# Planning the lists with loads in issue order and eight in flight, and giving twelve subtractions of the weight split to GpSimd

## The chip, the cores and the metric

The kernel runs on one NeuronCore of a Trainium2 chip. Its engines are TensorE (PE, with its weight loads as PEld), VectorE (DVE), ScalarE (ACT), GpSimd (POOL) and SyncE (SP), each with its own in-order list of instructions; they wait for each other through semaphores. SP issues most DMAs, POOL the loads of the attention's values. The metric is the device time of one execution in microseconds (us); the median of several runs is compared.

## What is computed

Attention in chunks, then two MLPs, all in float32:

```
chunk, left, right = 32, 16, 8          # q, k, v: 4 x 8 heads x 768 x 64; 8 memory rows
for each chunk c:
    k_full = [mem_k, k[c - left : c + chunk + right]];  v_full likewise
    a = softmax(q_c @ k_full.T / 8);    out_c = a @ v_full
x = out as 3072 x 512
g = s * relu(x @ w_in)**2 + b           # w_in 512 x 2048
x = g @ w_out                           # w_out 2048 x 512
y = (silu(x @ w_gate) * (x @ w_val)) @ w_out2   # 512 x 1536, 512 x 1536, 1536 x 512
```

## The kernel before, in words

**Tiles.** The 3072 tokens are eight tiles of 384 (t = 0 to 7), each made by three attention groups of 128 queries (g = 0 to 23). The first MLP's hidden width is cut into 16 slots (m). A slot is 128 columns of w_in and the 128 rows of w_out that belong to them, 1 MB in two DMAs (`load_slot`, lines 264 and 269), issued by SP.

**Exact products.** A float32 product is made of three fast ones: each operand is split into a high part and a rest (hi, lo), and `product` (lines 701 to 703) adds hi*hi, hi*lo and lo*hi. Splitting a slot (`split`, line 976) takes a chain of six: absolute value (`t_first`, ACT at line 985 or DVE at 987), bound (DVE, 991), shift (DVE, 995), sign (DVE, 1000), rest (DVE, 1007), the rounded copy hi (ACT or DVE, line 253 or 255), and the subtraction lo (`lo`, DVE, line 1049). All work on 128 x 1024 elements.

**The work by name.** The string START (line 30) orders PE's first work, one letter a piece: Q and K turn queries and keys of the first six groups, S makes scores, A turns probabilities (tile psA), V multiplies by values (psV), X turns the normalised result "on" (psO) into xhi and xlo, U is one slot's first product (hp) and D its second (acc). Each U or D is 12 matmuls of 384 columns. The pairs (t, m) of U and D go by SEGMENTS: m 0 to 3 of t = 0, then m 0 to 7 of t = 1, then the rest. So the fifth U, called U4 below, is the first of t = 1, and needs X3, X4 and X5, its groups' results.

**The planner.** The kernel writes its own schedule: `Plan.run` (line 116) plays the tasks against each other with the costs written beside them, and the order of starts in that play becomes the order of each engine's instructions. The chip then keeps that order and waits where a semaphore says so. Three tables feed it: START; LOADS (line 44), which chains the issues of the loads (BK and BQ keys and queries of the first groups, W slots, K6_n pieces of keys and queries for group 6); and MOVED (line 48), names of tasks that go to the second of their two engines (`either`, line 946: m_first is the absolute value, h_first hi, and so on).

A load is two tasks (`transfer`, line 953): the issue on SP and a transfer of so many kilobytes at a rate. The planner allows two such transfers in flight and starts the most urgent ready one first:

```
issue = issues[name] = plan.add(SP, 0.45 * n, emit, deps, [*get, "fly"], take=take)
return plan.add(MOVE, kilobytes / rate, None, [issue], put=["fly"], lag=1.8, give=give)
```

The values of a group are 8 to 10 DMAs issued by POOL (`load_values`, line 511; planned by `load_v`, line 958). Three buffers hold them in the first six groups: v0 for groups 0 and 3, v1 for 1 and 4, a lent slot "values" for 2 and 5. In the program as built, a DMA of SP waits for the one that stands eight places before it in SP's list, and likewise on POOL.

Of the kernel before, what the change touches and what calls it, by code (L numbers as in the profile page):

```python
# [29 lines left out]
START = (  # L30
    "K0 Q0 S0 Q1 A0 S1 S2 K1 V0 A1 S3 X0 V1 A2 X1 V2 A3 S4 X2 V3 U A4 S5 X3 U V4 A5 D X4 U D V5 "
    "U X5 D U D "
)
# [10 lines left out]
LOADS = (  # L44
    "BK0 C BM BK1 BQ01 BQ00 K6_0 BQ11 BQ10 W1 W0 W2 W3 W7 W4 W5 W12 W6 W8 W10 W9 W14 W11 W13 W15 "
)

MOVED = (
# [12 lines left out]
)  # L61


PAGE, FETCH = 256, ((45.0, 8.3), (110.0, 4.0), (1e9, 2.5))


class Plan:
# [32 lines left out]
    def after(d, t):  # L100

        return d.lag + (0.0 if d.engine == t.engine else 0.25)

    def end(self, t, now):

        left, rest = t.words, t.length
        while left:
            n = min(left, PAGE - self.word % PAGE)
            now, rest, left = now + rest * n / left, rest - rest * n / left, left - n
            self.word += n  # L110
            if self.word % PAGE == 0:
                now = max(now, self.next)
                self.next = now + (next(us for at, us in FETCH if now < at) if self.word > PAGE else 4.0)
        return now

    def run(self):
# [9 lines left out]
        heapq.heapify(events)  # L126
        ready = {t.engine: [] for t in self.tasks}
        free = dict.fromkeys(ready, True)
        started = []
        self.word, self.page, self.next = 0, 0.0, 0.0  # L130
        while events:
# [15 lines left out]
            for engine, waiting in ready.items():  # L147
                for item in sorted(waiting) if free[engine] else ():
                    t = self.tasks[item[1]]
                    if all(self.room[r] >= t.get.count(r) for r in t.get):  # L150
                        for r in t.get:
                            self.room[r] -= 1
                        waiting.remove(item)
                        free[engine] = False
                        t.start = now
                        started.append(t)
                        heapq.heappush(events, (self.end(t, now) if engine == "PE" else now + t.length, 0, t.n))
                        break
# [5 lines left out]
def attention_and_two_mlps(  # L164
# [467 lines left out]
    def stage_probs_copy(engine, g):  # L632
        staged[g]["at"] = at = ap_.tile([P, NC, P], F32, tag="at", name=f"at{g}")
        copy(engine, at, staged[g].pop("a"))
# [26 lines left out]

    def stage_normalise(g, e):
        if e == 0:
            staged[g]["on"] = ap_.tile([P, 4 * 2 * D], F32, tag="on", name=f"on{g}")
# [263 lines left out]
    def second_store(h, s, i):  # L928
# [7 lines left out]
    plan = Plan(  # L936
        dict(w=SLOTS - LENT, wt=SLOTS - 5, fly=2),
        dict(
# [14 lines left out]
    def transfer(deps, emit, n, kilobytes, get=(), take=(), give=(), rate=380.0, name=None):  # L953

        issue = issues[name] = plan.add(SP, 0.45 * n, emit, deps, [*get, "fly"], take=take)
        return plan.add(MOVE, kilobytes / rate, None, [issue], put=["fly"], lag=1.8, give=give)

    def load_v(g):
        first = g < VBUFS(0)
        n = 2 * (len(list(value_pieces(g))) + (first or (g >= EARLY and g % GB < VBUFS(g))))  # L960
        if f"V{g}" in LOADS.split():
# [3 lines left out]
            )  # L965
        else:
            issue = plan.add(
                "POOL", 9.2 if first else 0.65 * n, lambda: load_values(g, nc.gpsimd), [batch_landed["VM"]] if first else [],
                take=[f"vb{g % VBUFS(g)}"],
            )  # L970
            v_ = plan.add(MOVE, 1.8 if first else 2.4, None, [issue], lag=5.0 if first else 2.5)
        for e in range(2 if g >= EARLY and g % GB < VBUFS(g) else 0):
# [3 lines left out]
    def split(landed, raw, key, pool, name, done, put=("w",), sums=False):  # L976
# [176 lines left out]
    def plan_scores(g, t=None):  # L1153
# [34 lines left out]
        return t  # L1188

    def plan_probs(g, early):  # L1190
        ring = f"acc{2 + g % 2}" if early else "a"
# [7 lines left out]
        if g < EARLY:  # L1199
# [3 lines left out]
        at_[g]["at"] = either(  # L1203
            f"a{g}", {ACT: 0.50, DVE: 0.60}, lambda e: stage_probs_copy(e, g), [t], take=["at"],
            give=[ring],
        )

    x_parts = {}
    last_x = [None]

    def plan_values(g, t=None):
        d = at_[g]
        give = ["a"] if t is None else []
        if t is None:
            t = plan.add(
                PE, 1.30 if g < EARLY else 1.00, lambda: stage_values(g), [d["at"], d["v"]], take=["a", "a"],
                give=["at"] + [f"vb{g % VBUFS(g)}"] * (g not in (2, 5)), lag=0.2 if g < EARLY else 0.0,
                words=128,
# [9 lines left out]
        for e in range(2):  # L1228
            t = plan.add(
                DVE, 0.34, lambda e=e: stage_normalise(g, e), [t, d["rc"]], give=[*give, *([f"rc{g % 3}"] if e else [])],  # L1230
                take=["on"] if e == 0 else (),
            )
# [12 lines left out]
    def plan_turn(g):  # L1245
# [3 lines left out]
        if g < EARLY:  # L1249
            turned = plan.add(PE, 0.44, lambda: stage_turn(g), [d["on"]], take=["h"], give=["on"], lag=0.25, words=8)  # L1250
        else:
# [327 lines left out]
```

## Time and profile before

| | |
|---|---|
| median of the runs shown | 1216.6 us (1215.94, 1216.6, 1217.46) |
| the profiled execution | 1218.56 us |
| its span | 1216.8 us |
| PE busy | 1177.5 us, 97% |
| DVE busy | 750.3 us, 62% |
| ACT busy | 508.0 us, 42% |
| POOL busy | 146.5 us, 12% |
| DMA, mean | 144 GB/s |

The busy times are of the profiled execution alone, and its span begins with the first instruction. A row of a timeline gives the start in us from there, the duration, engine, source line, operation, destination and sources, the shape, how many were merged (x), and in brackets the idle time of that engine just before with what ended it. A row's duration can overlap the next one's start a little, as engines overlap the end of one instruction with the beginning of the next; differences of starts are free of this.

### The profile page before, as it was taken

The numbers are of one execution on the slowest core, as the hardware profiler recorded it, in microseconds if no ns is written. First come the engines' busy times: TensorE is split into PE (matmuls) and PEld (weight loads), VectorE is DVE, ScalarE is ACT, GpSimd is POOL, SyncE is SP. The second block draws the span as 40 slices with busy tenths as digits, with TensorE's granted clock in tenths as the row PEclk, the third lists the DMA queues.
The fourth block names the chain that finished last, engine by engine and source line by source line (L and its number), as shares of the span: only waits on it lengthen the run. The fifth ranks groups of instructions, "written<-read, shape, count | busy, mean of one in ns | idle before, by whom it ended". The sixth has DMA issues, their size and how long they took to land.

```text
span 1216.8 us, 23806 instructions
## 1 busy us (share of the span) xinstructions
PE 1177.5 (97%) x9440; PEld 1120.1 (92%) x9440; DVE 750.3 (62%) x1315; ACT 508.0 (42%) x924; POOL 146.5 (12%) x235
## 2 busy tenths in 40 slices
PE   6479999999999999999999999999999999999998
PEld 5379999999999999999999899999999999999997
DVE  6789976555455445444488965569853367743343
ACT  4445553233343433342276545346433234432332
POOL 4750013222222223120000000000000000000000
PEclk8699999999999999999999999999999999999999
DMA  9774235322222222220356265296565386465251
GB/s 296 161 196 135 79 95 105 68 45 65 40 55 66 45 64 48 46 54 2 113 201 231 110 228 216 118 323 251 196 228 216 115 331 248 156 250 207 105 207 52
DMA packets 160987, 175.42 MB, mean 144 GB/s; under 512 B 101276, under 2 KB 130252, under 8 KB 159852
## 3 DMA queue, kind: packets, MB, share of 16 engines
q1 hardware_dynamic: 153580, 162.54, 40.7%
q0 software_dynamic: 7296, 11.37, 4.1%
q8 instruction: 74, 1.21, 0.4%
q14 instruction: 37, 0.30, 0.1%
HBM read 124.85 MB, written 48.76 MB: 143 GB/s over the span
## 4 chain that ended last, share of the span: by engine, by line
PE 85%; SPq 5%; DMA 5%; DVE 4%; issue 1%; ACT 0%; DVEq 0%; ACTq 0%
PE hp L701 7%; PE acc L702 7%; PE acc L701 7%; PE acc L703 6%; PE hp L702 6%; PE hp L703 6%; PE chain_A L702 5%; PE oacc L703 5%; PE oacc L702 5%; PE chain_A L703 5%; PE chain_A L701 5%; PE oacc L701 5%; PE chain_B L701 4%; PE chain_B L703 4%; PE chain_B L702 4%; DMA kin<-in_k_dram 1%
## 5 line engine op out<-in xcount | busy, mean ns | idle before, releaser
L701 PE MATMUL hp<-xhi,w_first 128*128 128x384 f32 x512 | 174.3, 340 | 4.4 <-DVE xhi L255 4.4
L701 PE MATMUL acc<-ghi,w_first 128*128 128x384 f32 x512 | 173.1, 338 | 0.7 <-DVE ghi L754 0.3
L702 PE MATMUL hp<-xlo,w_first 128*128 128x384 f32 x512 | 172.0, 336 | 0.2 <-DVE xlo L696 0.2
L702 PE MATMUL acc<-glo,w_first 128*128 128x384 f32 x512 | 171.6, 335 | 0.6 <-DVE glo L761 0.4
L703 PE MATMUL hp<-xhi,w_first 128*128 128x384 f32 x512 | 171.8, 336 | 0.0
L703 PE MATMUL acc<-ghi,w_first 128*128 128x384 f32 x512 | 171.3, 334 | 0.0
L526 POOL DMA_DIRECT2D v<-in_v_dram x190 | 122.6, 652 | 306.9 <-PE psB L643 286.8
L871 ACT ACTIVATE kept<-chain_A 128x384 f32<-128x384 f32 x144 | 70.8, 492 | 187.4 <-PE chain_A L703 187.0
L702 PE MATMUL chain_A<-ops,hi_up 128*128 128x384 f32 x384 | 130.1, 339 | 0.0
L703 PE MATMUL chain_A<-ops,lo_up 128*128 128x384 f32 x384 | 129.4, 337 | 0.0
L701 PE MATMUL chain_A<-ops,hi_up 128*128 128x384 f32 x384 | 128.4, 334 | 0.9 <-ACT g L884 0.9
L741 DVE SCALAR_TENSOR_TENSOR r<-r,ident 128x384 f32<-128x384 f32 x91 | 55.8, 613 | 110.8 <-ACT r L730 110.2
L703 PE MATMUL oacc<-w_down,glo 128*128 128x512 f32 x288 | 114.6, 398 | 0.4 <-DVE glo L896 0.4
L702 PE MATMUL oacc<-w_down,ghi 128*128 128x512 f32 x288 | 113.9, 396 | 0.0
L730 ACT ACTIVATE r<-hp 128x384 f32<-128x384 f32 x94 | 46.1, 490 | 161.8 <-PE hp L703 156.0
L701 PE MATMUL oacc<-w_down,ghi 128*128 128x512 f32 x288 | 112.2, 390 | 0.2 <-ACT ghi L253 0.2
L701 PEld LDWEIGHTS hp<-xhi,w_first 128*128 128x128 f32 x512 | 96.5, 189 | 6.0 <-ACT t_first L985 4.7
L701 PEld LDWEIGHTS acc<-ghi,w_first 128*128 128x128 f32 x512 | 96.1, 188 | 2.0 <-DVE ghi L754 0.7
L702 PEld LDWEIGHTS acc<-glo,w_first 128*128 128x128 f32 x512 | 96.1, 188 | 1.8 <-DVE glo L761 1.0
L702 PEld LDWEIGHTS hp<-xlo,w_first 128*128 128x128 f32 x512 | 96.7, 189 | 0.7 <-DVE xlo L696 0.7
L876 DVE TENSOR_TENSOR kept<-chain_B,kept 128x384 f32<-128x384 f32 x48 | 26.7, 557 | 114.2 <-PE chain_B L703 114.2
L703 PEld LDWEIGHTS hp<-xhi,w_first 128*128 128x128 f32 x512 | 96.6, 189 | 0.0
(170 smaller groups left out, 2247.7 us busy)
## 6 DMA issues: line engine op xcount, KB each, us to landing
ops<-ops_dram SPq DMA_DIRECT2D x56, 768.0 KB
ops_dram<-ops SPq DMA_DIRECT2D x28, 768.0 KB
sum_dram<-o SPq DMA_DIRECT2D x48, 256.0 KB
v<-in_v_dram POOLq DMA_DIRECT2D x162, 56.0 KB, 3.0
raw_first<-in_moe_w_in_dram SPq DMA_DIRECT2D x16, 512.0 KB
raw_first<-in_moe_w_out_dram SPq DMA_DIRECT2D x16, 512.0 KB
o<-sum_dram SPq DMA_DIRECT2D x8, 1024.0 KB
y_dram<-y SPq DMA_DIRECT2D x32, 192.0 KB
```

What stands on the lines that cost most here:

```text
L526: queue.dma_start(out=tv[p0 + row:p0 + row + rows, c].rearrange("p (j d) -> p j d", d=D), in_=v[b, e:H:2, first:first + rows, :].rearrange ...
L701: nc.tensor.matmul(o, whi, xhi, start=first, stop=False, skip_group_check=onto)
L702: nc.tensor.matmul(o, whi, xlo, start=False, stop=False, skip_group_check=onto)
L703: nc.tensor.matmul(o, wlo, xhi, start=False, stop=last, skip_group_check=onto)
L730: nc.scalar.activation(out=r, in_=hp, func=AF.Relu)
L741: nc.vector.scalar_tensor_tensor(out=r, in0=r, scalar=s_sb, in1=r, op0=ALU.mult, op1=ALU.mult)
L871: nc.scalar.activation(out=t, in_=st2[n]["A"], func=AF.Copy)
L876: nc.vector.tensor_tensor(out=t, in0=st2[n]["B"], in1=kept, op=ALU.add)
```

## The change

- The planner's model: eight lanes for SP's loads instead of two transfers, held until landing; transfers start in the order in which they become ready; slots at 265 instead of 345 KB per us; POOL's values in two halves with lanes of their own; PE's instructions fetched at a cost that depends on the transfers that are waiting.
- START, LOADS and MOVED are written anew; so most orders of the first 150 us move.
- The subtraction lo of a first-MLP slot may go to POOL; MOVED sends twelve of the sixteen there: all but slots 0, 4, 11 and 15.
- In the first six groups, odd groups take their "at" and "on" tiles from buffers that lie idle then, so that two groups have one each; normalising (`stage_normalise`) may go to ACT, which MOVED does for group 0.

```diff
 START = (
-    "K0 Q0 S0 Q1 A0 S1 S2 K1 V0 A1 S3 X0 V1 A2 X1 V2 A3 S4 X2 V3 U A4 S5 X3 U V4 A5 D X4 U D V5 "
-    "U X5 D U D "
+    "Q0 K0 S2 S0 Q1 A0 S1 K1 V0 X0 S3 A1 A2 V1 V2 X1 A3 X2 S4 U S5 A4 U V3 A5 D X3 V4 U X4 V5 D "
+    "X5 U D U D "
 )
 LOADS = (
-    "BK0 C BM BK1 BQ01 BQ00 K6_0 BQ11 BQ10 W1 W0 W2 W3 W7 W4 W5 W12 W6 W8 W10 W9 W14 W11 W13 W15 "
+    "BQ01 BQ00 C BK1 BK0 BM BQ11 W0 K6_0 W2 BQ10 W1 K6_1 W3 K6_2 W4 W11 K6_3 W5 W6 W10 K6_4 W7 "
+    "W8 K6_5 K6_6 K6_7 K6_8 W12 W9 K6_9 K6_10 K6_11 W14 W13 W15 "
 )
 MOVED = (
...
+    "h_second17 h_second4 h_second5 k0_0 k0_2 k0_3 k1_0 k1_3 k2_1 k3_1 k7_0 k8_1 k9_1 l_first1 "
+    "l_first10 l_first12 l_first13 l_first14 l_first2 l_first3 l_first5 l_first6 l_first7 "
...
-PAGE, FETCH = 256, ((45.0, 8.3), (110.0, 4.0), (1e9, 2.5))
+PAGE, FETCH, QUEUED = 256, 3.7, 4.8
...
+    def queued(self, now):
+        rest = max(self.moved - now, 0.0) + sum(self.tasks[n].length for _, n in self.ready.get("MOVE", ()))
+        return min(rest, QUEUED)
...
-                self.next = now + (next(us for at, us in FETCH if now < at) if self.word > PAGE else 4.0)
+                self.next = now + FETCH + self.queued(now)
...
-                for item in sorted(waiting) if free[engine] else ():
+                for item in (list(waiting) if engine == "MOVE" else sorted(waiting)) if free[engine] else ():
...
     def stage_probs_copy(engine, g):
+        if g < EARLY and g % 2:
+            at = ap_.tile([P, H * KC], F32, tag="sc", name=f"at{g}").rearrange("p (c s) -> p c s", c=NC)
...
-    def stage_normalise(g, e):
+    def stage_normalise(g, e, engine="DVE"):
...
+        if engine == "ACT":
+            for j in range(NP):
+                nc.scalar.activation(
+                    out=on[:, (2 * j + e) * D:(2 * j + e + 1) * D], in_=o[:, j], func=AF.Copy, scale=rc[:, j]
+                )
+            return
...
-        dict(w=SLOTS - LENT, wt=SLOTS - 5, fly=2),
+        dict(w=SLOTS - LENT, wt=SLOTS - 5, fly=8, vly=10),
...
-        issue = issues[name] = plan.add(SP, 0.45 * n, emit, deps, [*get, "fly"], take=take)
-        return plan.add(MOVE, kilobytes / rate, None, [issue], put=["fly"], lag=1.8, give=give)
+        lanes = ["fly"] * min(n, 8)
+        issue = issues[name] = plan.add(SP, 0.45 * n, emit, deps, [*get, *lanes], take=take)
+        landed = plan.add(MOVE, kilobytes / rate, None, [issue], lag=1.8, give=give)
+        plan.add("NONE", 0.0, None, [landed], put=lanes)
+        return landed
...
-                "POOL", 9.2 if first else 0.65 * n, lambda: load_values(g, nc.gpsimd), [batch_landed["VM"]] if first else [],
+                "POOL", 0.32 * n, lambda: load_values(g, nc.gpsimd), [batch_landed["VM"]] if first else [], lanes,
...
-        def lo():
+        def lo(engine):
             w = done[key]
-            nc.vector.tensor_tensor(
+            (nc.gpsimd if engine == "POOL" else nc.vector).tensor_tensor(
                 out=w[:, 1], in0=held["f"].bitcast(F32), in1=w[:, 0].bitcast(F32), op=ALU.subtract
             )
...
-        return plan.add(DVE, 1.14, lo, [t], put=put)
+        return either(f"l_{name}", {DVE: 1.14, "POOL": 2.5}, lo, [t], put=put, lag=0.3)
```

What moves is seen best in three lists. The first is POOL's, from the loads for group 2 on. A name's first number is the group or the slot, so `w_first2` is slot 2's split; what follows the underline is a buffer's number. Before:

```order
L526 DMA values_215<-in_v_dram 56x4x64 x4
L526 DMA v0_213<-in_v_dram 56x4x64 x8
L526 DMA v1_431<-in_v_dram 56x4x64 x8
L526 DMA values_215<-in_v_dram 56x4x64 x3
L526 DMA values_215<-in_v_dram 48x4x64
L526 DMA values_215<-in_v_dram 8x4x64
```

With the change:

```order
L538 DMA v0_196<-in_v_dram 56x4x64 x8
L1081 TENSOR_TENSOR w_first1_643<-raw_first1_252,w_first1_643 128x1024
L538 DMA v1_420<-in_v_dram 56x4x64 x8
L538 DMA values_198<-in_v_dram 56x4x64 x3
L538 DMA values_198<-in_v_dram 48x4x64
L538 DMA values_198<-in_v_dram 8x4x64
L538 DMA values_198<-in_v_dram 56x4x64 x3
L538 DMA values_198<-in_v_dram 48x4x64
L538 DMA values_198<-in_v_dram 8x4x64
L1081 TENSOR_TENSOR w_first2_772<-raw_first2_212,w_first2_772 128x1024
L1081 TENSOR_TENSOR w_first3_1005<-raw_first3_394,w_first3_1005 128x1024
```

The subtraction of slot 1 now stands between the loads for groups 3 and 4, and those of slots 2 and 3 behind the ten loads for group 5.

The second is ACT's, around the absolute value of slot 4 and the xhi of group 0 or 1. Before:

```order
L253 ACTIVATE at1_663<-psA1_651 128x512
L985 ACTIVATE t_first4_701<-raw_first4_636 128x1024
L253 ACTIVATE xhi0_712<-psO0_704 128x4x128
L609 ACTIVATE values_215<-values_215 128x512
L985 ACTIVATE t_first5_777<-raw_first5_642 128x1024
L253 ACTIVATE w_first3_803<-raw_first3_352 128x1024
L253 ACTIVATE at2_816<-psA2_787 128x512
```

With the change:

```order
L265 ACTIVATE queries1_153<-psK1_2_555 128x12x56
L689 ACTIVATE on0_634<-psV0_0_592,rc0_456 128x64 x4
L689 ACTIVATE on0_634<-psV0_1_593,rc0_456 128x64 x4
L1017 ACTIVATE t_first4_708<-raw_first4_515 128x1024
L265 ACTIVATE at1_719<-psA1_703 128x512
L265 ACTIVATE at2_722<-psA2_712 128x512
L621 ACTIVATE values_198<-values_198 128x512
L265 ACTIVATE w_first2_772<-raw_first2_212 128x1024
L265 ACTIVATE xhi0_700<-psO1_815 128x4x128
```

Slot 4's absolute value stands behind group 0's normalising now, and slot 5's has left this stretch; it comes five places later, ahead of U0's relu.

The third is SP's, just ahead of slot 4's load. Before, the last nine of its rows there:

```order
L441 DMA kin0_193<-in_mem_k_dram 8x4x32
L432 DMA kin0_193<-in_k_dram 16x4x32
L432 DMA kin0_193<-in_k_dram 8x4x32
L451 DMA kin0_193<-in_k_dram 32x4x32
L455 DMA qt6_194<-in_q_dram 32x4x32
L451 DMA kin0_193<-in_k_dram 32x4x32
L455 DMA qt6_194<-in_q_dram 32x4x32
L264 DMA raw_first4_636<-in_moe_w_in_dram 128x4x256
L269 DMA raw_first4_636<-in_moe_w_out_dram 128x1024
```

With the change:

```order
L281 DMA raw_first3_394<-in_moe_w_out_dram 128x1024
L463 DMA kin0_173<-in_k_dram 32x4x32
L467 DMA qt6_174<-in_q_dram 32x4x32
L463 DMA kin0_173<-in_k_dram 32x4x32
L467 DMA qt6_174<-in_q_dram 32x4x32
L276 DMA raw_first4_515<-in_moe_w_in_dram 128x4x256
L281 DMA raw_first4_515<-in_moe_w_out_dram 128x1024
```

Slot 4 was the sixth slot, with fifteen pieces for group 6 just ahead of it; it is the fifth, with four just ahead. Slot 6 comes later in the list: thirty pieces for groups 6 and 7 follow slot 5 in a row, and then slot 6.

## Rows read from the trace of the kernel before

**Rows 1.** Busy time by stretches, columns as its first line names them.

```profile
core 0: us, PE busy (x) PEld busy (x) DVE busy (x) ACT busy (x) POOL busy (x), PEclk, DMA share, GB/s
0.00:89.00 89.00, 56.09 (x1197) 48.62 (x1197) 66.14 (x121) 40.19 (x95) 54.02 (x89) 0.83 0.84 218
89.00:600.00 511.00, 510.26 (x5035) 501.25 (x5036) 303.23 (x576) 202.59 (x365) 92.51 (x146) 1.00 0.28 66
45.00:53.00 8.00, 0.37 (x2) 0.00 (x0) 5.14 (x10) 2.71 (x4) 4.70 (x8) 0.50 1.00 187
```

**Rows 2.** Timeline of PE: start, us, what it did, idle before and its releaser.

```profile
44.26 1.11 PE L629 MATMUL psA<-ident,turned 128*128 128x128 f32 x4
53.07 1.13 PE L680 MATMUL psO<-ident,on 128*128 128x128 f32 x4 [7.70 <-DVE on L673]
...
72.71 0.63 PE L680 MATMUL psO<-ident,on 128*128 128x128 f32 x4
73.10 0.42 PE L701 MATMUL hp<-xhi,w_first 128*128 128x384 f32 x1
...
75.29 0.33 PE L701 MATMUL acc<-ghi,w_first 128*128 128x384 f32 x1
...
77.46 0.86 PE L643 MATMUL psV<-values,at 64*32 64x64 f32 x64
...
83.75 0.34 PE L703 MATMUL acc<-ghi,w_first 128*128 128x384 f32 x1
88.54 0.41 PE L701 MATMUL hp<-xhi,w_first 128*128 128x384 f32 x1 [4.45 <-DVE xhi L255]
...
92.61 0.34 PE L701 MATMUL acc<-ghi,w_first 128*128 128x384 f32 x1
```

**Rows 3.** Timeline of ACT, the same columns.

```profile
46.15 1.12 ACT L985 ACTIVATE t_first<-raw_first 128x1024 f32<-128x1024 f32 x1 [7.26 <-DMA raw_first<-in_moe_w_out_dram]
...
83.96 1.12 ACT L985 ACTIVATE t_first<-raw_first 128x1024 f32<-128x1024 f32 x1 [8.65 <-DMA raw_first<-in_moe_w_out_dram]
```

**Rows 4.** Timeline of DVE, the same columns.

```profile
47.79 0.69 DVE L696 TENSOR_TENSOR xlo<-psO,xhi 128x512 fp32r<-128x512 f32 x1 [4.73 <-ACT xhi L253]
...
85.11 0.69 DVE L991 TENSOR_SCALAR t_first<-t_first 128x1024 f32<-128x1024 f32 x1 [3.91 <-ACT t_first L985]
...
88.43 0.69 DVE L696 TENSOR_TENSOR xlo<-psO,xhi 128x512 fp32r<-128x512 f32 x1
```

**Rows 5.** Timeline of SyncE's queue (SPq): issues of loads.

```profile
38.58 0.55 SPq L264 DMA_DIRECT2D raw_first<-in_moe_w_in_dram  x1
...
52.36 0.31 SPq L451 DMA_DIRECT2D kin<-in_k_dram  x1
...
63.67 0.42 SPq L451 DMA_DIRECT2D kin<-in_k_dram  x1
...
77.41 0.56 SPq L264 DMA_DIRECT2D raw_first<-in_moe_w_in_dram  x1
```

**Rows 6.** Timeline of POOL.

```profile
1.02 0.29 POOL masks.py:199 TENSOR_SCALAR_AFFINE_SELECT ident<-ident 128x128 f32<-128x128 f32 x1
...
15.23 0.55 POOL L519 DMA_DIRECT2D v<-values  x1 [4.89 <-DMA values<-in_mem_v_dram]
...
52.84 3.48 POOL L526 DMA_DIRECT2D v<-in_v_dram  x5 [0.26 <-issue]
56.51 6.16 POOL L526 DMA_DIRECT2D values<-in_v_dram  x10 [0.19 <-PE psV L643]
```

**Rows 7.** Groups of DVE by line and shape, 0 to 95 us: count | busy us, mean ns.

```profile
L1049 DVE TENSOR_TENSOR w_first<-raw_first,w_first 128x1024 fp32r<-128x1024 f32 x6 | 7.3, 1219 | 0.1
...
L991 DVE TENSOR_SCALAR t_first<-t_first 128x1024 f32<-128x1024 f32 x8 | 5.4, 681 | 3.9 <-ACT t_first L985 3.9
```

**Rows 8.** Line 526, the loads of values on POOL, 0 to 80 us: ns min/median/max.

```profile
L526 POOL DMA_DIRECT2D v<-in_v_dram x52: 531/650/955, 15.8 to 77.5; - x52
...
DMA to landing us min/median/max: 2.1/4.4/8.1
```

More of the change, by code (lines that the diff above doesn't have):

```diff
@@ L126, in run @@
         heapq.heapify(events)
-        ready = {t.engine: [] for t in self.tasks}
+        self.ready = ready = {t.engine: [] for t in self.tasks}
         free = dict.fromkeys(ready, True)
         started = []
-        self.word, self.page, self.next = 0, 0.0, 0.0
+        self.word, self.next, self.moved = 0, 0.0, 0.0
         while events:
@@ L156, in run @@
                         started.append(t)
-                        heapq.heappush(events, (self.end(t, now) if engine == "PE" else now + t.length, 0, t.n))
+                        until = self.end(t, now) if engine == "PE" else now + t.length
+                        if engine == "VMOVE":
+                            until += 0.45 * self.queued(now)
+                        if engine == "MOVE":
+                            self.moved = until
+                        heapq.heappush(events, (until, 0, t.n))
                         break
@@ L632, in stage_probs_copy @@
     def stage_probs_copy(engine, g):
-        staged[g]["at"] = at = ap_.tile([P, NC, P], F32, tag="at", name=f"at{g}")
+        if g < EARLY and g % 2:
+            at = ap_.tile([P, H * KC], F32, tag="sc", name=f"at{g}").rearrange("p (c s) -> p c s", c=NC)
+        else:
+            at = ap_.tile([P, NC, P], F32, tag="at", name=f"at{g}")
+        staged[g]["at"] = at
         copy(engine, at, staged[g].pop("a"))
@@ L966, in load_v @@
         else:
+            lanes = ["vly"] * 5
             issue = plan.add(
-                "POOL", 9.2 if first else 0.65 * n, lambda: load_values(g, nc.gpsimd), [batch_landed["VM"]] if first else [],
+                "POOL", 0.32 * n, lambda: load_values(g, nc.gpsimd), [batch_landed["VM"]] if first else [], lanes,
                 take=[f"vb{g % VBUFS(g)}"],
             )
-            v_ = plan.add(MOVE, 1.8 if first else 2.4, None, [issue], lag=5.0 if first else 2.5)
+            v_ = plan.add("VMOVE", 1.2, None, [issue], put=lanes, lag=2.0)
+            issue = plan.add("POOL", 0.32 * n, None, [issue], lanes)
+            v_ = plan.add("VMOVE", 1.2, None, [issue, v_], put=lanes, lag=2.0)
         for e in range(2 if g >= EARLY and g % GB < VBUFS(g) else 0):
@@ L1188, in plan_scores, with at_ring @@
         return t
+    def at_ring(g):
+        return "own" if g < EARLY and g % 2 else "at"
     def plan_probs(g, early):
@@ L1203, in plan_probs @@
         at_[g]["at"] = either(
-            f"a{g}", {ACT: 0.50, DVE: 0.60}, lambda e: stage_probs_copy(e, g), [t], take=["at"],
+            f"a{g}", {ACT: 0.50, DVE: 0.60}, lambda e: stage_probs_copy(e, g), [t], take=[at_ring(g)],
             give=[ring],
@@ L1209, in attention_and_two_mlps, with on_ring @@
     last_x = [None]
+    def on_ring(g):
+        return "kt" if g < EARLY and g % 2 else "on"
     def plan_values(g, t=None):
@@ L1216, in plan_values @@
                 PE, 1.30 if g < EARLY else 1.00, lambda: stage_values(g), [d["at"], d["v"]], take=["a", "a"],
-                give=["at"] + [f"vb{g % VBUFS(g)}"] * (g not in (2, 5)), lag=0.2 if g < EARLY else 0.0,
+                give=[at_ring(g)] + [f"vb{g % VBUFS(g)}"] * (g not in (2, 5)), lag=0.2 if g < EARLY else 0.0,
                 words=128,
@@ L1228, in plan_values @@
         for e in range(2):
-            t = plan.add(
-                DVE, 0.34, lambda e=e: stage_normalise(g, e), [t, d["rc"]], give=[*give, *([f"rc{g % 3}"] if e else [])],
-                take=["on"] if e == 0 else (),
+            t = either(
+                f"n{g}_{e}", {DVE: 0.34, ACT: 0.80} if g < EARLY else {DVE: 0.34},
+                lambda engine, e=e: stage_normalise(g, e, engine), [t, d["rc"]],
+                give=[*give, *([f"rc{g % 3}"] if e else [])], take=[on_ring(g)] if e == 0 else (),
             )
@@ L1249, in plan_turn @@
         if g < EARLY:
-            turned = plan.add(PE, 0.44, lambda: stage_turn(g), [d["on"]], take=["h"], give=["on"], lag=0.25, words=8)
+            turned = plan.add(PE, 0.44, lambda: stage_turn(g), [d["on"]], take=["h"], give=[on_ring(g)], lag=0.25, words=8)
         else:
@@ L1269, in plan_w1 @@
         if m not in split1:
-            landed = transfer([], lambda: load_w1(m), 2, 1024, ["w", "w"], rate=345.0, name=f"W{m}")
+            landed = transfer([], lambda: load_w1(m), 2, 1024, ["w", "w"], rate=265.0, name=f"W{m}")
             split1[m] = split(landed, raw1, m, lambda: wp, f"first{m}", w1)
```

6 lines of the change are left out of this document (5 added, 1 removed), and 23 rows, old and new, of the table MOVED.

## Prediction

> **What bounds the kernel now.** I read the busy time by stretches first, to see where TensorE (PE) is not full. From 89 us to 600 us it is busy 510.26 of 511 us at full clock; in the first 89 us it is busy only 56.09 [rows 1]. What the change can win or lose lies in those first 89 us: behind them PE works through a fixed list without pause, so each microsecond by which it enters that list earlier comes off the end. The point of entry is U4, the first product of token tile 1, which starts at 88.54 us [rows 2].
>
> Next I read PE's instructions in order of time. Two of its waits are long. From the end of psA at 45.37 it stands until 53.07, 7.70 us, "on" being late on VectorE (DVE); and from 84.09 until 88.54, 4.45 us, xhi being late on DVE [rows 2]. In the first of them the granted clock is 0.50, the 1.2 GHz level, and PE was busy 0.37 of 8 us [rows 1].
>
> Then the same stretches on the engines that PE waits for. ScalarE (ACT) stands idle for 7.26 us before t_first at 46.15 and for 8.65 us before t_first at 83.96, each time for a load of raw_first [rows 3]. These are the absolute values of slots 4 and 6, which stand in ACT's queue before the load has come. Behind the first stands the xhi for which DVE idles 4.73 us; DVE itself idles 3.91 us for the second, with X5's xhi and xlo behind it in its queue [rows 4]. Last, SyncE's queue says why the loads are late: slot 4 is issued at 38.58, behind five other slots and fifteen pieces for group 6, and lands as ACT begins at 46.15; slot 6 is issued at 77.41 and lands by 83.96, 6.55 us later [rows 3, 5]. So PE is held by loads that an in-order queue asks for too soon, not by the load that PE needs next.
>
> **The change, part by part.** The rules of planning cost nothing by themselves: on the chip each load waits for the eighth before it in both programs. What runs differently is the order on each engine, twelve subtractions on GpSimd, four "at" and "on" tiles with buffers of their own, and group 0's normalising on ACT.
>
> *Loads.* Slot 4 is now the fifth slot to be loaded instead of the sixth, with the group 6 pieces between the slots, and its absolute value stands where ACT comes to it after group 0's normalising. I take both ACT stalls as gone: 4.73 + 3.91 = 8.6 us of DVE's idle time, and PE's two waits with them. The second is the closer call. In the change slot 6 is the load behind thirty small pieces, and its absolute value still stands one place ahead of X5's xhi on ACT. If slot 5 lands as late as the second slot of that pair did before (SyncE moves on at 52.36), and the 24 pieces that still wait then follow at the pace of the 23 from there to 63.67, 0.49 us each, slot 6 is issued at 64.2; with 6.55 us it lands at 70.7, and 1.1 + 0.7 + 0.7 us of ACT and DVE (absolute value, xhi at the price of xlo, xlo) put X5's xlo at 73.2 [rows 3 to 5]. That is hidden behind PE's own path (77.9, below) by 4.7 us.
>
> *DVE.* Up to X5's xlo DVE did 121 instructions, 66.14 us, so it idled 22.9 us of the 89 [rows 1, 4]. In the new order there are 112. The difference is four subtractions of slots fewer (4 x 1.22), two passes of the same size fewer (2 x 1.22), two short passes fewer and two rounding copies more, which I price alike (0.68 each; the copy has no row, the short pass is the nearest) [rows 7]; small instructions on both sides about cancel. That is 7.3 us. With 8.6 us of idle time gone X5's xlo would come at 89.1 - 7.3 - 8.6 = 73.2 us, if DVE alone set it.
>
> *GpSimd (POOL).* This is the new wait. POOL issued 56 loads of values between 15.23 and 62.67, at a median of 0.65 us each 36.4 us of work, with 11.0 us of waits for earlier ones to land [rows 6, 8]. Now the subtraction of slot 1 stands between group 3's loads and group 4's, and those of slots 2 and 3 behind the ten loads for group 5. No row shows a subtraction on POOL. Below, it can't be taken to beat DVE's 1.22 us; above, its affine select of 128 columns took 0.29 us [rows 6, 7], eight of those are 2.3 us, and reading two inputs instead of one could double that to 4.6. I take 2.3, the count by the nearest row. The Trainium skill (GPSIMD Engine Reference, Performance versus the Vector engine) has 4497 ns for 2048 columns, so an estimate of 2.25 us by halves; the sum would be the same within 0.1 us a piece.
>
> So slot 1's subtraction (2.3) puts the end of group 5's loads at 62.67 + 2.3 = 65.0, slot 2 is ready at 67.3, slot 3 at 69.6. PE's order now is U1, V3, A5, D0, X3, V4, U2, so U2 waits for slot 2: about 67.5. Without it PE would be there near 64, since V4 needs group 4's values, which were issued until 56.3, so now until 58.6, and land 4.4 us later, at 63.0 [rows 6, 8]. Behind U2 come X4, V5, D1, X5, U3, D2. From the rows: 2.19 + 0.39 + 0.86 + 2.17 + 0.39 + 2.19 + 2.17 = 10.4 us (differences of starts, and psV's own 0.86) [rows 2], with slot 3, group 5's values and X5's xlo all in time. U4 starts at 77.9 instead of 88.54: **10.6 us earlier**.
>
> *The clock.* U4 took from 88.54 to 92.61, 4.07 us instead of 2.19, at the lower level after PE's idle 4.45 us [rows 2]. In the change the waits before V4 and U2 sum to about as much, so I move this 1.9 us rather than drop it: 0 taken, 1.9 us the other end.
>
> *The rest.* Eight subtractions after U4 free DVE at a time when PE is full anyway; worth nothing as PE was busy 510.26 of 511 there. If they came late, PE would have new slots only from tile 1's fifth product, four pairs of 4.4 us after U4, and that is the cover. The buffers of "at" and "on" and the normalising on ACT (eight short activations instead of two of DVE's) stand within the stretch that POOL bounds: nothing.
>
> **Sum.** The profiled execution spans 1216.8 us, 1218.56 with what lies around it; 10.6 us off gives 1206.2 and 1208.0. The profiled run lay 2.0 over the median of the runs shown (1216.6), so the median comes to **1206.0 us**. A measurement of this kernel can tell about 0.2%, 2.4 us, from no change.
>
> **Rivals.**
> *POOL keeps up.* Its 11.0 us of waits shrink: the DMA engines' share is 1.00 between 45 and 53 [rows 1], where slots 4 and 5 will have come already. Then DVE's 73.2 is the bound, 15.3 us, and with a warm start 17.2: 1199.4. For it: those waits are for landings only. Against: the values are as many bytes.
>
> *DVE and POOL block each other.* No row of this kernel has POOL computing on tiles beside DVE. If DVE stands still through each subtraction, the four before X5's xlo (slots 1, 2, 3, 5) cost it 4 x 2.3 = 9.2 us: 73.2 + 9.2 = 82.4, so 6.1 us are won: 1210.5. The DVE passes at 1.22 us show no stretching beside POOL's issuing of loads [rows 7], which speaks neither way, as issuing reads no tile. The Trainium skill (SBUF — State Buffer, Who interferes with whom) says that a DVE instruction with two SBUF inputs and a GpSimd instruction that reads SBUF exclude each other for a whole instruction, the second one waiting. By that rule this rival is the likelier the more of DVE's passes read two SBUF tiles; here all of 1.22 us do. No row here shows it.
>
> *The wait for slot 6 stays.* At 0.9 us a piece instead of 0.63, slot 6 is issued at 74, and U4 starts at 82.9: 5.6 us, 1211.0. It decides from 0.69 us a piece on; the row gives 0.49.
>
> *No change.* The loads land later than this reckoning has them and the stalls stay in ACT's queue under other names, or several new waits add up to what went: 1214.2 to 1219. For it: with the slots' loads cut by pieces, each in line for the eighth before it, a late landing is passed on. Against: slots 4 and 5 have to come 10 us later than before, though less stands ahead of them.
>
> *Slower, through POOL.* Two subtractions stand in front of U2, so U4 is at 62.67 + 0.25 + 10.4 + 2s = 73.3 + 2s for a subtraction of s. It comes after 88.54 once s exceeds 7.6 us; at 9.2, four times what I take (two inputs read singly, and each held up by DVE as long again), U4 is at 91.7 and the time 1219.8. For it: PE has nothing else in its order until slot 2 is there. Against: no POOL row comes near that price.
>
> **How the numbers follow.** The forecast 0.50, POOL keeping up 0.14, the mutual block 0.13, slot 6 0.06, no change 0.09, slower 0.08. Faster by over 0.2% is the first four: 0.83; same 0.09; slower 0.08. The range leaves out the last two: from POOL keeping up, 1199.4, to the blocked cases, 1210.5 and 1211.0, with a second cold start of 1.9 us; the forecast with subtractions of 4.6 us (U4 at 82.5) lies inside. With the 0.7 to 0.9 us by which the runs shown differ from their median that is 1198.5 to 1213.5.
>
> **What would show it.** In the new profile: U4 near 78 us; ACT without a wait of 7 us for raw_first; a wait of PE before U2 that ends with POOL's w_first at about 67; POOL's subtraction near 2.3 us. DVE's passes well over 1.22 us beside POOL's subtractions would show the block. It is wrong if PE waits again for xhi behind a t_first of ACT, if POOL's subtraction lasts over 5 us, or if PE has idle time behind U4 that it did not have.

## The result, and the profile after

| | before | changed |
|---|---|---|
| median of the runs | 1217.03 us (4 runs) | 1227.07 us (4 runs) |
| ratio to before, 95% interval | | 1.0084 (1.0069 to 1.0099) |
| the profiled execution, its span | 1218.56, 1216.8 us | 1226.94, 1225.2 us |
| DVE busy | 750.3 us | 760.7 us |
| POOL busy | 146.5 us | 176.4 us |

The change makes the kernel about 10 us slower. The forecast was 1206.0 us, 1198.5 to 1213.5.

The busy times by stretches, after (the first three answer to [rows 1]; columns as there):

```profile
0.00:89.00 89.00, 61.10 (x1219) 53.65 (x1220) 70.00 (x118) 39.83 (x89) 62.05 (x90) 0.83 0.87 218
89.00:600.00 511.00, 500.87 (x4966) 489.04 (x4966) 304.81 (x556) 201.01 (x354) 114.35 (x158) 1.00 0.26 61
45.00:53.00 8.00, 4.85 (x75) 3.84 (x74) 4.19 (x6) 1.11 (x2) 6.91 (x9) 0.50 0.58 114
100.00:160.00 60.00, 53.02 (x351) 49.53 (x350) 57.80 (x73) 28.55 (x43) 14.79 (x6) 1.00 0.35 107
```

The last of these stretches in the kernel before, which the prediction did not look at:

```profile
100.00:160.00 60.00, 59.99 (x406) 59.29 (x405) 57.36 (x86) 33.39 (x61) 0.00 (x0) 1.00 0.36 109
```

In the first 89 us PE does 5.0 us more work than before, as hoped. From 89 to 600 us it does 9.4 us less, and 7.0 of that lies between 100 and 160. DVE is busy 57.80 of those 60 us; before it was busy 57.36 of 60 and PE was still full. So DVE was all but full there before too, and only just in time.

PE in order of time, after (to be read beside [rows 2]; psO at 74.43 is X4, in front of V5; 84.31 is U4):

```profile
74.43 1.13 PE L706 MATMUL psO<-ident,on 128*128 128x128 f32 x4 [5.15 <-DVE on L699]
...
84.31 0.33 PE L727 MATMUL hp<-xhi,w_first 128*128 128x384 f32 x1
...
87.32 0.45 PE L728 MATMUL acc<-glo,w_first 128*128 128x384 f32 x1 [0.59 <-DVE glo L787]
...
94.51 0.44 PE L727 MATMUL acc<-ghi,w_first 128*128 128x384 f32 x1 [2.92 <-DVE ghi L267]
...
96.52 0.52 PE L727 MATMUL acc<-ghi,w_first 128*128 128x384 f32 x1
```

U4 comes 4.2 us earlier than before, and at the 2.4 GHz level (granted clock 1.00 from 84.31 to 86.39). Behind it PE waits for ghi and glo, which it did not do there before (no such wait from 84 to 200 us); after the wait that ends at 94.51 a matmul takes 0.52 us for a while instead of 0.33, and the granted clock between 94.5 and 98.5 is 0.63, most of it the 1.2 GHz level, so that one wait costs about 1.9 us more than its length (this acc runs 3.9 us from 94.51 to 98.44, a usual one 2.08). By the first psB (the attention of a later group, a landmark in PE's list) the 4.2 us won at U4 have become 9.6 us lost. Before, then after:

```profile
165.22 0.91 PE L643 MATMUL psB<-v,at 64*32 64x64 f32 x64
```

```profile
174.81 0.85 PE L659 MATMUL psB<-v,at 64*32 64x64 f32 x61
```

In the whole trace no wait of PE ends with a subtraction of POOL, so it is not that POOL delivers late.

The reason stands in two timelines laid side by side. POOL's subtractions, after:

```profile
50.62 2.44 POOL L1081 TENSOR_TENSOR w_first<-raw_first,w_first 128x1024 fp32r<-128x1024 f32 x1
...
64.42 5.33 POOL L1081 TENSOR_TENSOR w_first<-raw_first,w_first 128x1024 fp32r<-128x1024 f32 x2
...
82.01 2.44 POOL L1081 TENSOR_TENSOR w_first<-raw_first,w_first 128x1024 fp32r<-128x1024 f32 x1
...
88.56 2.65 POOL L538 DMA_DIRECT2D v<-in_v_dram  x4
91.22 2.41 POOL L1081 TENSOR_TENSOR w_first<-raw_first,w_first 128x1024 fp32r<-128x1024 f32 x1
...
105.49 2.44 POOL L1081 TENSOR_TENSOR w_first<-raw_first,w_first 128x1024 fp32r<-128x1024 f32 x1 [3.62 <-ACT w_first L265]
113.92 2.51 POOL L1081 TENSOR_TENSOR w_first<-raw_first,w_first 128x1024 fp32r<-128x1024 f32 x1 [6.00 <-ACT w_first L265]
```

And DVE at those times:

```profile
50.50 0.76 DVE L699 TENSOR_TENSOR on<-psV,rc 128x256 f32<-128x256 f32 x2 [3.81 <-PE psV L659]
51.17 2.44 DVE L1027 TENSOR_SCALAR t_first<-t_first 128x1024 uint32<-128x1024 uint32 x1
...
59.03 0.17 DVE L675 TENSOR_SCALAR rc<-rc 128x8 f32<-128x8 f32 x1
...
65.33 2.13 DVE L767 SCALAR_TENSOR_TENSOR r<-r,ident 128x384 f32<-128x384 f32 x1
67.38 0.67 DVE L672 TENSOR_REDUCE rc<-queries 128x8 f32<-128x512 f32 x1
68.08 1.69 DVE L675 TENSOR_SCALAR rc<-rc 128x8 f32<-128x8 f32 x1
...
80.97 0.69 DVE L722 TENSOR_TENSOR xlo<-psO,xhi 128x512 fp32r<-128x512 f32 x1
81.58 3.96 DVE L1032 SCALAR_TENSOR_TENSOR raw_first<-raw_first,t_first 128x1024 uint32<-128x1024 uint32 x1
...
89.52 4.66 DVE L1027 TENSOR_SCALAR t_first<-t_first 128x1024 uint32<-128x1024 uint32 x1
94.11 0.35 DVE L267 CAST ghi<-r 128x384 fp32r<-128x384 f32 x1
...
105.72 2.63 DVE L767 SCALAR_TENSOR_TENSOR r<-r,ident 128x384 f32<-128x384 f32 x1
...
114.21 2.64 DVE L789 SCALAR_TENSOR_TENSOR glo<-r,ident,ghi 128x384 fp32r<-128x384 f32 x1
```

A shift that takes 0.69 us elsewhere took 2.44 and 4.66; passes of SCALAR_TENSOR_TENSOR (STT) over 384 columns, 0.62 us elsewhere, took 2.13 to 2.64; a pass over 8 columns, 0.17 us at 59.03, took 1.69. Each ends 0.03 to 1.1 us after a subtraction of POOL ends. The ghi for which PE waits until 94.51 stands right behind the 4.66 us. The twelve passes so held were together 24.6 us too long, 7.5 us of it in four that began before U4 and 17.1 us in eight after it: 2.05 us for each subtraction, where the same subtraction on DVE takes 1.22 us [rows 7]. Relieving DVE of 12 x 1.22 = 14.6 us cost it 24.6; the balance, +10.0, is nearly the +10.4 us of DVE's busy time in the table. Passes that read PSUM ("on" at 50.50) and the reduction at 67.38 were not held.

### The profile page after: what moved, and what is told of

The parts are those of the page before. It is cut to its first block, busy times and chain, and to the rows that moved or that the text cites. A ratio compares the mean times of both kernels' runs of the same rounds, so it can differ in the third digit from the quotient of the medians.

```text
span 1225.2 us, 23815 instructions
## 1 busy us (share of the span) xinstructions
PE 1181.7 (96%) x9440; PEld 1121.3 (92%) x9440; DVE 760.7 (62%) x1300; ACT 507.5 (41%) x910; POOL 176.4 (14%) x247
## 4 chain that ended last, share of the span: by engine, by line
PE 80%; DVE 7%; DMA 5%; SPq 5%; issue 2%; ACT 1%; POOL 0%; DVEq 0%; ACTq 0%; POOLq 0%
PE acc L727 6%; PE acc L728 6%; PE acc L729 6%; PE hp L727 6%; PE hp L728 6%; PE hp L729 6%; PE chain_A L728 5%; PE oacc L729 5%; PE oacc L728 5%; PE chain_A L729 5%; PE chain_A L727 5%; PE oacc L727 5%; PE chain_B L727 4%; PE chain_B L728 4%; PE chain_B L729 4%
## 5 line engine op out<-in xcount | busy, mean ns | idle before, releaser
L756 ACT ACTIVATE r<-hp 128x384 f32<-128x384 f32 x103 | 50.5, 490 | 161.3 <-PE hp L729 157.9
L727 PEld LDWEIGHTS acc<-ghi,w_first 128*128 128x128 f32 x512 | 96.7, 189 | 5.9 <-DVE ghi L267 3.9
L727 PEld LDWEIGHTS hp<-xhi,w_first 128*128 128x128 f32 x512 | 96.3, 188 | 1.4 <-issue 0.2
L729 PEld LDWEIGHTS acc<-ghi,w_first 128*128 128x128 f32 x512 | 96.8, 189 | 0.0
```

The lines of the kernel that those rows point to most:

```text
L727: nc.tensor.matmul(o, whi, xhi, start=first, stop=False, skip_group_check=onto)
L729: nc.tensor.matmul(o, wlo, xhi, start=False, stop=last, skip_group_check=onto)
L756: nc.scalar.activation(out=r, in_=hp, func=AF.Relu)
```

## Experiments

Theory HOLD is that of these two timelines: a DVE pass that meets a subtraction of GpSimd stands until that has ended. Its rivals: ORDER, that the new lists leave DVE too much to do after U4, whoever subtracts; LOADS, that slots land late. Ratios are to the kernel before on the same chip, with 95% intervals; "psB" is the landmark named above.

| run | ratio (interval) | U4, us | first psB, us |
|---|---|---|---|
| the kernel before | 1 | 88.54 | 165.22 |
| the change | 1.0084 (1.0069 to 1.0099) | 84.31 | 174.81 |
| all_on_dve | 0.9967 (0.9954 to 0.9979) | 84.63 | 164.62 |
| late_8_on_dve | 1.0005 (0.9995 to 1.0015) | 86.22 | 167.13 |
| early_4_on_dve | 1.0018 (1.0009 to 1.0028) | 84.37 | 170.06 |
| before_12_pool | 1.0092 (1.0078 to 1.0106) | 86.40 | 176.78 |
| nobody_subtracts | 0.9909 (0.9895 to 0.9923) | 79.49 | 154.17 |
| before_nobody | 1.0006 (0.9996 to 1.0016) | 90.62 | 167.50 |
| pool_in_quarters | 1.0050 (1.0038 to 1.0063) | 82.94 | 171.57 |
| pool_copies | 0.9952 (0.9939 to 0.9965) | 81.51 | 160.45 |
| pool_fills | 0.9941 (0.9919 to 0.9962) | 81.86 | 162.40 |
| dve_replanned | 0.9966 (0.9954 to 0.9978) | 82.51 | 159.65 |
| act_takes_copies | 0.9950 (0.9937 to 0.9963) | 82.54 | 161.05 |
| act_replanned | 0.9961 (0.9947 to 0.9976) | 82.52 | 159.21 |

U4 and psB are read from one profiled execution each. From psB to the end of the span the kernel before falls another 1.1 to 1.2 us behind the lists of the change (9.6 us become 8.4; with nobody subtracting a lead of 11.1 becomes 12.2), so psB is best compared between runs with the same lists.

### Who subtracts, with the order kept

```diff
-            (nc.gpsimd if engine == "POOL" else nc.vector).tensor_tensor(
+            nc.vector.tensor_tensor(
```

> The changed kernel with every order kept, and the twelve subtractions issued to DVE at the very places in the program where GpSimd had them. Theory HOLD (a GpSimd subtraction stops a DVE instruction that starts beside it until it ends): in the changed kernel the passes held between 84 and 160 us lasted 18.6 us too long in all for eight subtractions, those before U4 about 7.5 us for four; on DVE the twelve cost 9.8 and 4.9 us. So DVE gains about 9 us after U4 and 2.6 before; U4 near 82, PE waits after U4 down from 12.7 us to about 4, time 1213 to 1219. Rival ORDER (the new lists leave DVE with more of the split to do after U4, whoever subtracts): DVE has 14.6 us more to do, so 1227 or more, up to 1235. Rival LOADS (slots land late): no change, 1226 to 1228.

Measured 0.9967: 0.0117 below the change, 14.2 us of 1217. PE's waits after U4, until 200 us (us in total, times, longest):

```profile
PE acc L728 <- DVE glo L787: 1.9, 3, 1.5
PE acc L728 <- DVE glo L789: 0.2, 1, 0.2
```

In the change the same view was:

```profile
PE acc L728 <- DVE glo L789: 5.0, 5, 2.2
PE acc L727 <- DVE ghi L267: 3.2, 2, 2.9
PE acc L728 <- DVE glo L787: 1.8, 5, 0.6
PE acc L727 <- DVE ghi L780: 0.6, 1, 0.6
```

ORDER and LOADS fall: one word in one line takes the loss away, and DVE is faster with 14.6 us more to do. U4 did not come at 82 but at 84.63, so the gain lies behind U4. The expectation had counted the pass at 81.58 on both sides of U4: the eight holds behind it come to 17.1 us and not 18.6, and only three of the four before it stand ahead of X5's xlo (80.97).

The same done for eight or four of the twelve, `key not in {6, 7, 8, 9, 10, 12, 13, 14}` or `key not in {1, 2, 3, 5}` added to the condition:

> The changed kernel with the same orders; the subtractions of slots 1, 2, 3 and 5 (before U4) stay on GpSimd, those of slots 6 to 10 and 12 to 14 (after U4) are issued to DVE in place. HOLD: U4 stays at 84.3, the PE waits after it shrink by 18.6 - 9.8 = 8.8 us; 1217 to 1220. ORDER: DVE has 9.8 us more to do in the stretch where PE waits for it, 1227 to 1237. LOADS: 1226 to 1228.

> The changed kernel with the same orders; the subtractions of slots 1, 2, 3 and 5 are issued to DVE in place, the eight after U4 stay on GpSimd. HOLD: DVE is 2.6 us better off before U4, which comes at 81 to 83 instead of 84.3, but the eight holds after it stay, and the PE waits after U4 with them (11 to 15 us); 1224 to 1227. ORDER: U4 4.9 us of DVE work later or the same, 1227 to 1232.

The first came as HOLD has it (1.0005), with U4 later than expected: here one DVE pass was held through both subtractions for slots 2 and 3, 6.77 us for a pass of 1.23:

```profile
63.66 6.77 DVE L1039 SCALAR_TENSOR_TENSOR raw_first<-raw_first 128x1024 uint32<-128x1024 uint32 x1
```

The second missed: 1.0018 where 1.006 to 1.008 was expected, and U4 at 84.37 where 81 to 83 was. With the order of events a little shifted, the subtraction of slot 6 met a pass that it held for 0.9 us and not 4.0, and the 2.9 us wait with its slow stretch was not there. So what a hold costs seems to hang on which pass it meets; the two halves save 9.6 and 8.0 us, together 14.2.

### Only the twelve subtractions, in the kernel before

```diff
+            here = name.startswith("first") and key in {1, 2, 3, 5, 6, 7, 8, 9, 10, 12, 13, 14}
-            nc.vector.tensor_tensor(
+            (nc.gpsimd if here else nc.vector).tensor_tensor(
```

> The kernel before with nothing changed but the engine of the subtractions of the same twelve slots, GpSimd instead of DVE, each where it stood in the program. HOLD: DVE passes of 0.6 to 1.23 us become 2 to 4 us beside them, DVE loses about 1.1 us a piece more than it is relieved of; DVE was 95% busy from 100 to 160 us without a wait of PE, so PE waits for ghi and glo appear there, and the time is 1221 to 1229. ORDER or LOADS: DVE has 14.6 us less to do, no new waits of PE; 1212 to 1217.

1.0092, as HOLD has it. Passes held there, from DVE's timeline:

```profile
93.08 2.51 DVE L754 TENSOR_SCALAR ghi<-r,ident 128x384 fp32r<-128x384 f32 x1
95.62 2.63 DVE L763 SCALAR_TENSOR_TENSOR glo<-r,ident,ghi 128x384 fp32r<-128x384 f32 x1
```

Moving the subtractions costs some 11 us in the old order too; the loss needs nothing else of the change.

### Nobody subtracts: what the forecast took for granted

In `lo` the twelve subtractions are not issued, and `weight1` gives the high half twice:

```diff
-        return w[:, 0, n * 512:(n + 1) * 512], w[:, 1, n * 512:(n + 1) * 512]
+        low = 0 if f"l_first{m}" in moved else 1
+        return w[:, 0, n * 512:(n + 1) * 512], w[:, low, n * 512:(n + 1) * 512]
```

> The changed kernel with the same orders, in which the twelve subtractions that GpSimd did are left out: for these slots TensorE reads the high half in place of the low half, with the same number of matmuls. This is what the forecast took for granted: DVE is neither burdened nor held. HOLD: against the kernel with all on DVE, DVE is relieved of 14.6 us, PE's waits for ghi and glo after U4 are gone (below 1 us), U4 comes at 78 to 82, and the ratio to before is 0.988 to 0.993 (1205 to 1210 on the scale of 1217). Rival BOUND (DVE's other work or the landing of slots holds U4 and PE anyway): U4 stays at 83 to 85, waits of PE stay at 2 us or more, ratio 0.996 to 0.998 as with all on DVE.

0.9909, which is 1206.0 us on 1217. U4 comes at 79.49, PE has no wait for ghi or glo behind it, and the lead at psB is 11.1 us, all of U4's 9.05 and the slow start of U4 before:

```profile
100.00:160.00 60.00, 59.96 (x524) 58.92 (x523) 50.24 (x82) 30.08 (x48) 5.14 (x8) 1.00 0.31 85
```

DVE is at 50.24 of 60 us here. So the forecast's sum is about that of a kernel in which GpSimd's subtraction costs DVE nothing. That both come to 1206.0 is partly luck: U4 is 9.05 us earlier here and not 10.6, and the slow start of U4 before, 1.9 us, which the forecast took to come back elsewhere, is won as well.

The same edit in the kernel before, with its own lists:

> The kernel before, with its own orders, in which the subtractions of the same twelve slots are left out (TensorE reads the high half in place of the low half, with the same number of matmuls). It tells what the new lists are worth beside the relief of DVE. LISTS: the waits of 7 us for raw_first on ACT stay, U4 stays at 86 to 88.5, and as TensorE is full behind it the ratio to before is 0.997 to 1.000, while the new lists with nobody subtracting gave 0.991. RELIEF: the 14.6 us less on DVE do it all, U4 comes at 79 to 82 and the ratio is 0.990 to 0.994.

1.0006, and U4 at 90.62, later than either theory had it: with 14.6 us less on DVE and the old lists nothing is won. The waits stay, on ACT (as in [rows 3]) and on PE (as in [rows 2]):

```profile
47.92 1.12 ACT L989 ACTIVATE t_first<-raw_first 128x1024 f32<-128x1024 f32 x1 [7.55 <-DMA raw_first<-in_moe_w_out_dram]
...
86.04 1.12 ACT L989 ACTIVATE t_first<-raw_first 128x1024 f32<-128x1024 f32 x1 [8.76 <-DMA raw_first<-in_moe_w_out_dram]
```

```profile
54.87 1.14 PE L684 MATMUL psO<-ident,on 128*128 128x128 f32 x4 [10.72 <-DVE on L677]
...
90.62 0.66 PE L705 MATMUL hp<-xhi,w_first 128*128 128x384 f32 x1 [5.48 <-DVE xhi L258]
```

What takes those stalls away is the rest of the change (loads, START, buffers, normalising on ACT; these were not tried one by one). The rest and the relief are worth 11 us together, the relief alone nothing, the rest alone (all_on_dve) 4.

### What holds what

Four pieces in place of one subtraction:

```diff
+            for c in (slice(a, a + CH // 4) for a in range(0, CH, CH // 4)) if engine == "POOL" else ():
+                nc.gpsimd.tensor_tensor(
+                    out=w[:, 1, c], in0=held["f"][:, c].bitcast(F32), in1=w[:, 0, c].bitcast(F32), op=ALU.subtract
+                )
```

> The changed kernel with the same orders and each subtraction of GpSimd cut into four of 256 columns. HOLD by instruction: a DVE pass waits for the end of the piece that runs when it starts, at most 0.7 us, so no pass is held for 2 us or more; DVE passes get in between the pieces, each piece can hold one, so the sum of holds falls by less than half and the time lies between all on DVE and the change: 1218 to 1226 on the scale of 1217, ratio 1.001 to 1.007. Rival HOLD FOR THE RUN (DVE stays out as long as GpSimd has such work in its queue): passes are held 2 us and more as before, ratio 1.008 or more.

1.005. Most passes beside the pieces are held by about 0.5 us each, one after the other, but two stay out for several pieces: 2.55 us for 0.69 at 86.22, and the last line here, 3.1 us over its usual 0.42, where under 2 was expected:

```profile
95.89 1.23 DVE L1027 TENSOR_SCALAR t_first<-t_first 128x1024 uint32<-128x1024 uint32 x1
97.16 1.67 DVE L1032 SCALAR_TENSOR_TENSOR raw_first<-raw_first,t_first 128x1024 uint32<-128x1024 uint32 x1
98.86 1.66 DVE L1039 SCALAR_TENSOR_TENSOR raw_first<-raw_first 128x1024 uint32<-128x1024 uint32 x1
...
110.52 3.55 DVE L780 TENSOR_SCALAR ghi<-r,ident 128x384 fp32r<-128x384 f32 x1
```

The pieces also came late themselves: in U2 PE waited 3.02 us for POOL's w_first, until 70.44. So this run does not show the price of the holds alone.

Other work in the subtraction's place, `nc.gpsimd.tensor_copy(w[:, 1], held["f"].bitcast(F32))` or `nc.gpsimd.memset(w[:, 1].bitcast(F32), 0.0)`:

> The changed kernel with the same orders, GpSimd copying the slot's 1024 columns into the low half in place of subtracting (the subtraction is left out for twelve slots; one tile is read instead of two). HOLD through any SBUF work of GpSimd: DVE's two-input passes and its passes over one SBUF tile are held as long as the copy lasts; a copy of 1.2 to 2.4 us puts the ratio between 1.000 and 1.008. Rival HOLD THROUGH TWO INPUTS ALONE: no DVE pass is stretched, and the ratio is that of the kernel where nobody subtracts, 0.988 to 0.993.

> The changed kernel with the same orders, GpSimd filling the low half with zeros in place of subtracting (the subtraction is left out for twelve slots; GpSimd reads no tile, it only writes). If it is reading that holds DVE: no pass is stretched; ratio as where nobody subtracts, 0.988 to 0.993. If writing holds too: DVE's one-input passes of 0.69 us (bound, shift, casts) are stretched by up to the fill's length, the two-input passes (sign, STT of r and glo) not; ratio 0.993 to 1.002. If every DVE pass is held by any GpSimd work: both kinds are stretched.

The copy lasts 1.10 to 2.12 us on POOL, 1.13 at the median and so shorter than expected, and holds both kinds of passes: a shift of 0.69 us took 1.43, and of the passes with two SBUF inputs, 0.62 and 0.56 us elsewhere,

```profile
103.61 1.17 DVE L767 SCALAR_TENSOR_TENSOR r<-r,ident 128x384 f32<-128x384 f32 x1
...
110.35 1.18 DVE L787 TENSOR_TENSOR glo<-r,ghi 128x384 fp32r<-128x384 f32 x1
```

So GpSimd's work need not have two inputs for the hold. At 0.9952 the run is faster than expected: the passes held beside the copies are together about 6 us too long, not 24.6.

The fill, 0.96 us, comes at other times than the subtraction, as it reads nothing. It does not hold the pass with two SBUF inputs at 103.07 that starts while it runs, nor those at 66.20 and 79.12, but it holds a cast from SBUF to SBUF, here through five fills in a row (POOL's rows, then DVE's):

```profile
87.03 4.54 POOL L1082 MEMSET w_first<- 128x1024 f32 x5
102.77 0.96 POOL L1082 MEMSET w_first<- 128x1024 f32 x1 [11.20 <-ACT w_first L265]
```

```profile
86.81 4.97 DVE L267 CAST ghi<-r 128x384 fp32r<-128x384 f32 x1
...
103.07 0.62 DVE L767 SCALAR_TENSOR_TENSOR r<-r,ident 128x384 f32<-128x384 f32 x1
```

PE waits 3.6 us for that one ghi in the profiled execution, which took 1214.75 us. Of the other three, one took 1215.13 us and two took 1207.96 and 1208.31, which is the 0.991 of nobody_subtracts; that this one hold makes the difference is likely but not shown, as those two left no trace.

### A faster version

The change without the twelve names, planned anew; and, with the subtractions on DVE in the places of the change, seven short passes moved to ACT, which is busy 28.64 of the 60 us from 100 to 160 in all_on_dve:

> The change without the twelve names in MOVED: the planner knows that DVE subtracts and writes its orders accordingly; loads, START and everything else as in the change. HOLD: no pass of DVE is stretched; time as with all on DVE in the old places or a little better, ratio 0.993 to 0.998. ORDER (the new lists cost): 1.000 or more.

```diff
-            if engine == ACT:
+            if engine == ACT or name in {"first7", "first9", "first15"}:
...
+            engine = ACT if name in {"first11", "first12", "first14", "first15"} else engine
             copy(engine, done[key][:, 0], held["f"].bitcast(F32))
```

> All on DVE in the places of the change, and seven passes of 0.69 us of slots 7, 9, 11, 12, 14 and 15 (three absolute values, four rounded copies) issued to ACT in place of DVE. If DVE is the bound between 84 and 160 us, as the waits of PE for glo and its 95% say, 4.8 us less on DVE take most of the 2.3 us of PE's waits after U4 away: ratio 0.994 to 0.997, against 0.9967 for all on DVE. Rival: ACT's copies come later than DVE's did and hold the split up, ratio 0.998 or more.

> The same engines as in the run where ACT takes the seven passes, but with orders that the planner writes for them. If the planner's orders fit the chip, a little better than that run, 0.992 to 0.996; if its orders put an ACT copy behind a load that lands late, as before, 0.997 to 1.002.

All three beat both kernels. act_takes_copies has the lowest ratio, 0.9950, but its interval meets those of the others and of all_on_dve, so their order and the worth of the seven passes stay open; and the reason expected for it was only partly met: PE is busy 58.53 of 60 us from 100 to 160 (57.70 in all_on_dve), while its waits for ghi and glo are 2.0 us against 2.1, and 2.1 us of its lead stand at U4 already, ahead of the first pass that was moved (slot 7's absolute value, at 85.61 in all_on_dve), so the edit did not make those. The two planned anew stand 1.4 and 1.8 us ahead of it at psB and lose that again at a wait for a slot, so act_replanned is not the little faster that was expected:

```profile
170.27 0.63 PE L727 MATMUL hp<-xhi,w_first 128*128 128x384 f32 x1 [3.08 <-ACT w_first L265]
```

In their lists on SyncE one slot's load less stands ahead of the second store of y, which is issued at 120.30 us in act_replanned; that this makes the slot late was not tried.

## Why the prediction was wrong

**Right: the stalls of ACT and their cause.** Up to 100 us no t_first on ACT waits over 1.7 us for its load in the changed kernel (7.26 and 8.65 before [rows 3]). Slot 6 is issued even earlier than the forecast's 64.2:

```profile
58.36 0.56 SPq L276 DMA_DIRECT2D raw_first<-in_moe_w_in_dram  x1
```

(The 0.63 us a piece that the rival of slot 6 names stands in no row; the pace of its sum is 0.49.) And before_nobody shows that in the old lists the stalls stay though DVE has less to do.

**Right: POOL's price. Luck: the time of U2.** A subtraction took 2.41 to 2.78 us (forecast 2.3). U2 came at 66.93 (forecast 67.5), but the wait for POOL's w_first that was to set it is not there, and in nobody_subtracts, without any subtraction, U2 is at 66.69. So POOL was not the new wait, and the rival "Slower, through POOL" named the direction and not the way.

**Wrong: "That is 7.3 us", the saving on DVE up to X5's xlo.** It counted what DVE no longer does and not what it waits. The four subtractions there saved 4.9 us, and ahead of X5's xlo three passes were held 4.8 us, so as good as nothing was left of it: all_on_dve, which does the four itself, has U4 at 84.63 against 84.31. The step behind it failed too, "with slot 3, group 5's values and X5's xlo all in time": it left out X4's "on". Behind U2 PE waited 5.15 us for that, with a slow stretch after it (granted clock 0.50 from 74.43 to 78.40), and U4 came at 84.31, not 77.9. Without any subtraction 2.02 us of the wait stay and U4 is at 79.49:

```profile
71.09 0.72 PE L707 MATMUL psO<-ident,on 128*128 128x128 f32 x4 [2.02 <-DVE on L700]
```

So of the 6.4 us that were missing at U4, 4.8 come with the subtractions and 1.6 were missing without them.

**Wrong, and the larger part: "Eight subtractions after U4 free DVE at a time when PE is full anyway; worth nothing".** PE was full there, and DVE was at 57.36 of 60 us beside it: the step read PE's row and not DVE's. Eight holds of 17.1 us in place of 9.8 us of subtractions turned that into 7.0 us of PE's idle time from 100 to 160 us, and 3.7 more with a slow stretch before.

**Wrong: "each microsecond by which it enters that list earlier comes off the end".** This holds in nobody_subtracts, where DVE has 50.24 of 60 us to do. In all_on_dve U4 is 3.9 us earlier and has no slow start, and of these 5.8 us 0.6 are left at psB and 1.7 at the end of the span: PE that comes earlier waits for glo, with DVE busy 55.21 of the 60 us from 100 to 160. (The ratio, of medians, has 4.0 us; the traces do not show the rest.)

**The rival named the mechanism and not its size.** "DVE and POOL block each other" had 0.13 and 1210.5 us. It let DVE stand still for four subtractions before X5's xlo, and charged nothing for the eight behind. With those at the measured balance, 17.1 - 9.8 = 7.3 us, and 1.9 for the slow stretch, it would have been at 1219.7, still 7.4 us short of the measured time, as PE lost more behind U4 than DVE's balance; how that comes about in full is open. I gave it little because no row had POOL computing beside DVE, and because I asked only for passes with two SBUF inputs; the held shifts and casts have one. The Trainium skill (SBUF — State Buffer, Who interferes with whom) names those too: copies, casts and tensor_scalar passes in modes that use both ports exclude GpSimd's work, passes with two SBUF inputs exclude only GpSimd work that reads SBUF, and tensor_reduce on this chip does neither. The trace agrees on each: shift 2.44 for 0.69, a pass with two SBUF inputs 2.63 for 0.62 beside a subtraction but 0.62 beside a fill, the reduction 0.67 as ever.

## What to carry to other kernels

Before work goes from DVE to GpSimd, compare what DVE is relieved of with the time that GpSimd takes for it, not with nothing: here 1.22 us was given to an engine that took 2.44 and kept DVE out for 2.05 on average. An engine that keeps PE just fed has no slack to be freed: read the row of every engine in a stretch in which PE is full. Where a helper is wanted, ACT took seven passes, and no pass of DVE was stretched; whether that by itself made the kernel faster is not shown.

## What was not expected of the hardware

- A DVE pass can be held from before the GpSimd subtraction begins in the trace: the shift of 4.66 us started at 89.52, while POOL was issuing four loads (88.56 to 91.21), and the subtraction is recorded from 91.22. It did not happen each time; why is open, and POOL's spans in the profile are rough.
- Several GpSimd instructions in a row can hold one DVE pass through all of them (6.77 us through two subtractions, 4.97 through five fills), though in pool_in_quarters DVE mostly got in between. What decides it was not tried.
- On POOL a copy of 128 x 1024 with one input takes 1.13 us at the median and a subtraction with two 2.47, more than double.
